# A convolution kernel: the second weight block's first sums moved ahead of the first unit's adds on GpSimd, and the first unit's silus moved back on ScalarE

## The chip, the cores and the metric

The kernel runs on one core of a Trainium2 chip. The core has TensorE (matmul; PE in the profile, its weight loads are PEld), VectorE (DVE), ScalarE (ACT), GpSimd (POOL) and SyncE (SP, which here issues nearly all DMAs). Each engine works through its own queue in order and waits on semaphores for the others. The metric is the device time of one execution in microseconds (us), as the median of several runs.

## What is computed

A one-dimensional convolution of width 3 over the sequence, a batch norm with given statistics, and a silu. B = 2 images, S = 2048 rows, C = 1024 channels in and out, bf16:

```
xp = jnp.pad(x, ((0, 0), (1, 1), (0, 0)))
y = sum(jnp.einsum('bsc,cd->bsd', xp[:, k:k + S, :], w[k]) for k in range(3))
y = (y - mean) * (g / jnp.sqrt(var + 1e-5)) + b
out = y * sigmoid(y)
```

## The kernel before, in words

The convolution is done by a fast algorithm of Winograd's kind. Six rows of the output (R = 6) come from eight products (NJ = 8), one for each of the points 0, 1, -1, 2, -2, 1/2, -1/2 and infinity, numbered 0 to 7 in this order. The image is transformed once by matmuls with a small constant matrix (`t_job`, L282 to L303; the results are cast from PSUM to SBUF by ScalarE or VectorE into `T_sb`). The weights are transformed block by block.

**Weights.** The 1024 output channels are 8 blocks `dc` of 128. For each block the three taps w0, w1, w2 lie in `raw[dc]`. `even_part` (L163) makes a sum e0 = w0 + w2, e1 = 4 w2 + w0 or e2 = 4 w0 + w2 in fp32. It does so on GpSimd in one `tensor_tensor` (L169) or on VectorE in one `scalar_tensor_tensor` with the factor 4 in it (L171). `transform_w` (L184, instruction at L190) makes on GpSimd the two signs of each pair: u0 = e0 +- w1, u1 = e1 +- 2 w1, u2 = e2 +- 2 w1. The doubled tap 2 w1 comes from `double_w` (L154), on ScalarE at L157, in a buffer named `w1x2`, of which there are two. Below, u1+ and u1- are the two signs of u1, and so on. u0 belongs to the points +-1, u1 to +-2 and u2 to +-1/2. Each sum and each sign is one instruction over 128 x 1024 elements.

`prepare_w(dc)` (L192) queues e0, u0+ and u0- at once, and leaves three jobs: the doubling for ScalarE (`act_work`), and e1 with u1, and e2 with u2 (`dve_work`), which `idle` takes off one by one at fixed places of later units. `prepare_first(0)` (L208) does the first block, all on GpSimd but the doubling.

**Units.** A unit is one block of output channels times one image; there are 16, in the order (block 0, image 0), (block 0, image 1), (block 1, image 0) and so on: unit 0, 1, 2, 3. Even units use PSUM banks 0 to 3, odd ones 4 to 7. Each of a unit's eight products is eight matmuls (one for each 128 input channels, L336), and is written here as (bank, number of the point), as in the call `self.product(q, j, ...)`; the bank is counted within the unit's four. A unit's order (`run`, L439) is (3,1), copy of bank 3; (0,3), copy of bank 0 times 4; (3,2), copy of bank 3; (0,4); (2,5), copy of bank 2; (2,6). The copies are ScalarE's (L347, L349). VectorE's combinations (`combine`, L354) turn the banks into the six output rows: t0, t1 and t2 from the low pair of banks, then four more behind (2,6). Two rows stand in banks 1 and 2, two in t1 (in SBUF), and two in banks 0 and 3, to which the products of point 0 and of infinity, (0,0) and (3,7), are added in the next unit. So, from unit 1 on, (3,7) of unit n runs between (2,5) and (2,6) of unit n + 1, and (0,0) behind (2,6). The silus (L359, ScalarE) read the banks and write `yT`; a DMA transpose (L524, SP) and stores follow.

**Places.** `run` calls `behind(n)` at numbered places: 1 behind the first copy, 4 behind (0,4), 5 behind the copy of bank 2 (the copy of point 5), 6 at the end. What is left of the unit before is given as a list of (place, function). As every engine's queue is in program order, this is a place in each engine's queue.

**Unit 0** (`run_first`, L384) is another: its (3,0) and (0,7) come first and are copied to `ends`, GpSimd adds these to t0 and t2 (L410, L411) once VectorE has made t0 and t2, and the image transforms of the second image run between its products. Right behind the two adds, `prepare_w(1)` (L412) puts e0, u0+ and u0- of block 1 into GpSimd's queue; at the unit's end `idle(act_work)` and `idle(dve_work)` (L421, L422) give ScalarE the doubling and VectorE e1. VectorE makes e2 in the middle of unit 1 (L469). Unit 0's silus are unit 1's affair (`rest_first`, L424): the two inner ones (t1 and banks 1 and 2) at place 4, the outer one (banks 0 and 3) at place 5. Unit 2 is the first to use block 1 and, after unit 0, the first to use banks 0 to 3 again.

Of the kernel before, what the change touches and what calls it, by code (L numbers as in the profile page):

```python
# [9 lines left out]
ALU = mybir.AluOpType  # L10
FP32 = mybir.dt.float32
BF16 = mybir.dt.bfloat16
# [3 lines left out]
P = 128  # L16
R = 6
# [9 lines left out]
def kernel(  # L27
# [10 lines left out]
    nc = tc.nc  # L38
    B, S, C = x.shape
    D = w.shape[2]  # L40
    CT, DC = C // P, D // P
# [9 lines left out]
    epool = ctx.enter_context(tc.tile_pool(name="epool", bufs=1))  # L51
    spool = ctx.enter_context(tc.tile_pool(name="spool", bufs=2))
# [12 lines left out]
    ps = pspool.tile([P, 8, 512], FP32, name="ps")  # L65
# [46 lines left out]
    def ends(e, size):  # L112
        return max(clock[e], clock["pe"] + 100.0) + cost[e][0] * size + cost[e][1]

    def busy(e, size):
        clock[e] = ends(e, size)
# [13 lines left out]
    raw, wts = {}, {}  # L130
# [3 lines left out]
    def load_w(pair, k, half=None):  # L134

        if (pair, "tile") not in raw:
            raw[pair, "tile"] = wpools[pair % 2].tile([P, 3, CT, 2, P], BF16, name=f"wch{pair % 2}")
        wch = raw[pair, "tile"]
        h0, h1 = (0, 2) if half is None else (half, half + 1)
        cols = slice((2 * pair + h0) * P, (2 * pair + h1) * P)  # L140
        nc.sync.dma_start(
            out=wch[:, k, :, h0:h1].rearrange("p c h d -> p c (h d)"), in_=w_all[:, k, :, cols]
        )
        clock["dma"] += 1400.0 * (h1 - h0)
        for h in range(2):
            raw[2 * pair + h] = wch[:, :, :, h]

    double, sums, act_work, dve_work = {}, {}, [], []

    def idle(work):  # L150
        if work:
            work.pop(0)()

    def double_w(dc, eng):  # L154
        t = spool.tile([P, CT, P], BF16, name="w1x2")
        if eng is nc.scalar:
            nc.scalar.mul(t, raw[dc][:, 1], 2.0)  # L157
            busy("act", CT * P)
        else:
            eng.tensor_scalar(t, raw[dc][:, 1], 2.0, 0.0, op0=ALU.mult, op1=ALU.add)  # L160
        double[dc] = t

    def even_part(dc, q, eng, by=None):  # L163

        w0, w2 = raw[dc][:, 0], raw[dc][:, 2]
        e = epool.tile([P, CT, P], FP32, name=f"e{q}")
        f, h = (w2, w0) if q == 1 else (w0, w2)
        if q == 0:
            eng.tensor_tensor(e, w0, w2, op=ALU.add)  # L169
        elif eng is nc.vector:  # L170
            eng.scalar_tensor_tensor(out=e, in0=f, scalar=4.0, in1=h, op0=ALU.mult, op1=ALU.add)  # L171
        else:
            t = spool.tile([P, CT, P], BF16, name="w1x2")
            if by is nc.scalar:
                by.mul(t, f, 4.0)
                busy("act", CT * P)
            else:
                by.tensor_scalar(t, f, 4.0, 0.0, op0=ALU.mult, op1=ALU.add)
            eng.tensor_tensor(e, t, h, op=ALU.add)
        if eng is nc.vector:  # L180
            busy("dve", CT * P)
        sums[dc, q] = e

    def transform_w(dc, q, signs=(0, 1)):  # L184

        o = double[dc] if q else raw[dc][:, 1]
        if (dc, q) not in wts:
            wts[dc, q] = upool.tile([P, 2, CT, P], BF16, name=f"u{q}")
        for i in signs:
            nc.gpsimd.tensor_tensor(wts[dc, q][:, i], sums[dc, q], o, op=(ALU.add, ALU.subtract)[i])  # L190

    def prepare_w(dc):  # L192

        even_part(dc, 0, nc.gpsimd)
        transform_w(dc, 0)

        def second():
            even_part(dc, 1, nc.vector)
            transform_w(dc, 1)

        def third():
            even_part(dc, 2, nc.vector)
            transform_w(dc, 2)

        act_work.append(lambda: double_w(dc, nc.scalar))
        dve_work.extend((second, third))

    def prepare_first(dc):  # L208
# [20 lines left out]

        return left  # L230

    prm = consts.tile([P, 4, DC], BF16, name="prm")
    scale = consts.tile([P, DC], FP32, name="scale")
    beta = consts.tile([P, DC], FP32, name="beta")
# [77 lines left out]
    class Unit:  # L312
# [54 lines left out]
        def first(self, between):  # L367

            self.product(0, 0, True, between)
            self.silu(0, self.bank[0])  # L370
# [10 lines left out]
            self.product(3, NJ - 1, True, between)  # L381
            self.silu(slice(0, R, R - 1), ps[:, self.b0:self.b0 + 4:3, self.lo:self.hi])

        def run_first(self, between, left, prepare):  # L384


            b0, b1, b2, b3 = self.bank
            sd = dpool.tile([P, 2, NB], FP32, name="sd")
            t0 = dpool.tile([P, 2, NB], FP32, name="t0")
            t2 = dpool.tile([P, 2, NB], FP32, name="t2")  # L390
            ends = dpool.tile([P, 2, NB], FP32, name="ends")
            self.y23 = t1 = ypool2.tile([P, 2, NB], FP32, name="t1")
            left()
            self.product(3, 0, False, between)
            self.copy(3, dst=ends[:, 0])
            self.product(0, NJ - 1, False, between)
            self.copy(0, dst=ends[:, 1])
            clock["pe"] = max(clock["pe"], T_FIRST)
            self.product(3, 1, False, between)
            pa = self.copy(3)  # L400
            self.product(0, 3, False, between)
            pb = self.copy(0, by=4.0)
            self.product(3, 2, True, between)
            self.copy(3, dst=sd[:, 0])
            self.combine(sd[:, 1], pa, 2.0, b3, ALU.subtract)
            self.product(0, 4, True, between)
            self.combine(b1, b0, -2.0, pb)
            for t, a in ((t0, -0.0125), (t2, -0.2), (t1, -0.05)):
                self.combine(t, self.low, a, sd)
            nc.gpsimd.tensor_tensor(t0[:, 0], t0[:, 0], ends[:, 0], op=ALU.add)  # L410
            nc.gpsimd.tensor_tensor(t2[:, 1], t2[:, 1], ends[:, 1], op=ALU.add)  # L411
            prepare_w(prepare)  # L412
            self.product(2, 5, False, between)
            pc = self.copy(2)
            between.rest()
            self.product(2, 6, True, between)
            self.combine(b3, b2, -0.5, pc)
            self.combine(self.low, self.high, -1.6, t0)
            self.combine(t1, self.high, -0.4, t1)
            self.combine(self.high, self.high, -0.1, t2)  # L420
            idle(act_work)  # L421
            idle(dve_work)  # L422

        def rest_first(self):  # L424

            return [
                (4, self.silu_inner),
                (5, lambda: self.silu(slice(0, R, R - 1), ps[:, self.b0:self.b0 + 4:3, self.lo:self.hi])),
            ]

        def rest(self, between, last=5, first=6):
# [118 lines left out]
    left = []  # L550
# [39 lines left out]
    between = Between()  # L590
# [3 lines left out]
    for i, (dc, bi) in enumerate(seq[:-1]):  # L594
        unit = Unit(dc, bi, i % 2 * 4)
        if i == 0:
            unit.run_first(between, left[0], 1)
        else:
            unit.run(
                between,  # L600
                prev.rest_first() if i == 1 else prev.rest(between, *((4, 5) if i >= len(seq) - 3 else (5, 6))),
                2 if i == 2 else dc + 2 if bi == 1 and 0 < dc < DC - 2 else None,
            )
        if i == 0:
            xwin_scope.close()
            olast = ctx.enter_context(tc.tile_pool(name="olast", bufs=3))
            wpools[1] = ctx.enter_context(tc.tile_pool(name="wpool1", bufs=1))
        if i in (0, 4, 8):
            for k in range(3):
                load_w(i // 4 + 1, k)  # L610
        if i == len(seq) - 2:
            prev.turn(olast, ((1, R), (0, 1)))
        elif prev:
            prev.turn()
        if before:
            before.store(late if i == len(seq) - 2 else ())
        before, prev = prev, unit
    before.store(late)
    dc, bi = seq[-1]
# [45 lines left out]
```

## Time and profile before

| | us |
|---|---|
| median of 3 runs | 192.54 |
| lowest, highest | 192.10, 192.76 |
| the profiled execution, its own time | 192.87 |
| its span, first to last instruction | 191.0 |
| TensorE busy | 178.2 (93%) |
| VectorE busy | 159.5 (84%) |
| GpSimd busy | 145.3 (76%) |
| ScalarE busy | 110.2 (58%) |

All durations come from the one profiled execution; 1.9 us of its time lie outside the span. Its mean granted TensorE clock is 0.999 of full speed. A row of a timeline shows start, length, engine, line, operation, tile written and tiles read, shape, and the count of instructions merged into it; brackets show the idle time ahead and what released the engine.

### The profile page before, as it was taken

What the parts mean: (1) busy time and instruction counts of PE and PEld (TensorE: products, weight loads), DVE (VectorE), ACT (ScalarE), POOL (GpSimd) and SP (SyncE); (2) the same over time, 40 slices, a digit from 0 to 9 for tenths busy, and PEclk for the clock granted to TensorE, in tenths of its full rate; (3) what the DMA queues carried; (4) which work ended last, traced back from release to release, by engine and by line L of the source; (5) the groups of instructions that cost most, each with busy time, mean ns of one, the idle gap of its engine ahead of it and who ended that gap; (6) DMA issues with size and microseconds to landing.
All of it is one profiled execution on the core that took longest, in us unless ns stands there. A gap on an engine that the chain in (4) does not pass through costs nothing.

```text
span 191.0 us, 3722 instructions
## 1 busy us (share of the span) xinstructions
PE 178.2 (93%) x1402; PEld 125.0 (65%) x1402; DVE 159.5 (84%) x214; ACT 110.2 (58%) x180; POOL 145.3 (76%) x86
## 2 busy tenths in 40 slices
PE   6969999998679999999999999999999999999991
PEld 2758688775336666666666666666666666669880
DVE  5548667899996999999998899889978897678781
ACT  3689698677118383638354745465455647363790
POOL 3377999179999779999999999999999973021122
PEclk9999999999999999999999999999999999999999
DMA  5999999056600939299597593994783958767935
GB/s 155 335 346 332 378 357 216 2 164 172 124 0 0 155 84 191 56 307 188 111 185 136 114 210 108 257 206 80 160 165 85 209 58 189 146 139 139 196 75 110
DMA packets 86958, 31.72 MB, mean 166 GB/s; under 512 B 73542, under 2 KB 82778, under 8 KB 86940
## 3 DMA queue, kind: packets, MB, share of 16 engines
q1 hardware_dynamic: 85820, 31.24, 71.3%
q10 hardware_dynamic: 864, 0.21, 0.5%
q8 instruction: 11, 0.18, 0.4%
q0 software_dynamic: 256, 0.03, 0.2%
q14 instruction: 7, 0.06, 0.1%
HBM read 14.82 MB, written 8.39 MB: 122 GB/s over the span
## 4 chain that ended last, share of the span: by engine, by line
PE 76%; POOL 6%; DMA 5%; DVE 5%; issue 3%; SPq 2%; ACT 1%; DVEq 0%; POOLq 0%
PE ps L336 71%; DMA xw<-in_x_dram 5%; PE ps L290 5%; POOL u L190 4%; DVE T_sb L303 4%; SPq L125 2%; POOL e L169 1%; ACT T_sb L301 1%; PE ps L495 1%; POOL t L411 0%; DVE t L354 0%; POOL t L410 0%; ACT yT L359 0%; DVEq L660 0%; DVE ps L354 0%
## 5 line engine op out<-in xcount | busy, mean ns | idle before, releaser
L336 PE MATMUL ps<-T_sb,u 128*128 128x342 bf16 (+2 forms) x816 | 120.7, 299 | 3.7 <-POOL u L190 2.5
L336 PEld LDWEIGHTS <-u 128*128 128x128 bf16 x816 | 76.4, 97 | 37.9 <-POOL u L190 4.2
L190 POOL TENSOR_TENSOR u<-e,w1x 128x1024 bf16<-128x1024 f32 x32 | 70.3, 2223 | 3.8 <-DVE e L171 2.5
L336 PE MATMUL ps<-T_sb,wch 128*128 128x342 bf16 (+2 forms) x272 | 43.0, 299 | 0.4 <-ACT T_sb L301 0.4
L190 POOL TENSOR_TENSOR u<-e,wch 128x1024 bf16<-128x1024 f32 x16 | 39.6, 2495 | 1.9 <-DMA wch<-in_w_dram 1.3
L359 ACT ACTIVATE yT<-ps,beta,scale 128x342 bf16<-128x342 f32 (+4 forms) x49 | 33.7, 719 | 11.0 <-PE ps L336 10.9
L354 DVE SCALAR_TENSOR_TENSOR t<-ps,sd 128x684 f32<-128x684 f32 (+2 forms) x51 | 39.1, 821 | 0.6
L347 ACT COPY pc<-ps 128x342 f32<-128x342 f32 (+2 forms) x34 | 14.5, 427 | 34.2 <-PE ps L336 33.5
L336 PEld LDWEIGHTS <-wch 128*128 128x128 bf16 x272 | 25.6, 97 | 11.8 <-issue 0.7
L171 DVE SCALAR_TENSOR_TENSOR e<-wch 128x1024 f32<-128x1024 bf16 x14 | 32.8, 2341 | 0.0
L303 DVE CAST T_sb<-ps 128x1008 bf16<-128x1008 f32 (+2 forms) x20 | 22.1, 1121 | 11.9 <-PE ps L290 11.8
L301 ACT CAST T_sb<-ps 128x1008 bf16<-128x1008 f32 (+2 forms) x30 | 24.9, 866 | 7.3 <-PE ps L290 7.1
L354 DVE SCALAR_TENSOR_TENSOR ps<-ps,t 128x684 f32<-128x684 f32 (+2 forms) x34 | 28.3, 832 | 0.7
L290 PE MATMUL ps<-rm,xw 128*128 128x168 bf16 (+2 forms) x272 | 25.3, 235 | 2.5 <-DMA xw<-in_x_dram 1.9
L290 PEld LDWEIGHTS <-xw 128*128 128x128 bf16 (+2 forms) x272 | 20.6, 99 | 8.6 <-DMA xw<-in_x_dram 3.3
L354 DVE SCALAR_TENSOR_TENSOR ps<-ps,pc 128x342 f32<-128x342 f32 (+2 forms) x34 | 16.8, 494 | 7.8 <-PE ps L336 6.7
L169 POOL TENSOR_TENSOR e<-wch 128x1024 f32<-128x1024 bf16 x7 | 16.9, 2412 | 0.0
L359 ACT ACTIVATE yT<-t,beta,scale 128x684 bf16<-128x684 f32 (+2 forms) x17 | 15.7, 925 | 0.0
L354 DVE SCALAR_TENSOR_TENSOR t<-ps,t 128x684 f32<-128x684 f32 (+2 forms) x17 | 13.9, 818 | 0.0
L349 ACT ACTIVATE pc<-ps 128x342 f32<-128x342 f32 (+2 forms) x17 | 7.5, 441 | 11.1 <-PE ps L336 8.3
L537 POOL DMA_DIRECT2D out_dram<-o x2 | 1.4, 712 | 15.7 <-DMA o<-yT 15.7
L347 ACT COPY sd<-ps 128x342 f32<-128x342 f32 (+2 forms) x17 | 7.3, 429 | 10.2 <-PE ps L336 10.2
(51 smaller groups left out, 55.9 us busy)
## 6 DMA issues: line engine op xcount, KB each, us to landing
xw<-in_x_dram SPq DMA_DIRECT2D x32, 256.0 KB
out_dram<-o SPq DMA_DIRECT2D x28, 192.0 KB
wch<-in_w_dram SPq DMA_DIRECT2D x9, 512.0 KB
out_dram<-o SPq DMA_DIRECT2D x14, 120.0 KB
wch<-in_w_dram SPq DMA_DIRECT2D x6, 256.0 KB
out_dram<-o SPq DMA_DIRECT2D x3, 128.0 KB
o<-yT SPq DMA_TRANSPOSE x15
out_dram<-o SPq DMA_DIRECT2D x12, 7.5 KB
```

The source lines that it names most:

```text
L125: nc.sync.dma_start(out=xw[0:hi - lo, :], in_=x[bi, lo:hi, :])
L169: eng.tensor_tensor(e, w0, w2, op=ALU.add)
L171: eng.scalar_tensor_tensor(out=e, in0=f, scalar=4.0, in1=h, op0=ALU.mult, op1=ALU.add)
L190: nc.gpsimd.tensor_tensor(wts[dc, q][:, i], sums[dc, q], o, op=(ALU.add, ALU.subtract)[i])
L290: nc.tensor.matmul(v[:, q, c], lhsT=xw[0:rows, (c0 + c) * P:(c0 + c + 1) * P], rhs=mat[0:rows, :, 0:n], start=True, stop=True,)
L301: nc.scalar.copy(dst, src)
L303: nc.vector.tensor_copy(dst, src)
L336: nc.tensor.matmul(self.bank[q], lhsT=lhsT, rhs=T_sb[self.bi][:, ct, j, nsl], start=not add and ct == 0, stop=ct == CT - 1, skip_group_che ...
L347: nc.scalar.copy(dst, self.bank[q])
L349: nc.scalar.mul(dst, self.bank[q], by)
L354: nc.vector.scalar_tensor_tensor(out=out, in0=in0, scalar=scalar, in1=in1, op0=ALU.mult, op1=op1)
L359: nc.scalar.activation(self.yT[:, rows, self.lo:self.hi], src, ACT.Silu, bias=beta[:, dc:dc + 1], scale=scale[:, dc:dc + 1])
```

## The change

Three things move, all for block 1, whose weights unit 2 uses first. A new function `prepare_second(1)` takes the place of `prepare_w(1)` and returns four jobs.

- GpSimd: e0 and u0+ stand in front of the two adds of L410 and L411, and u0- behind them.
- e1 is made on GpSimd, as one `tensor_tensor` of w0 and a buffer `g` = 4 w2; ScalarE makes `g` at the end of unit 0, where it made the doubled tap. The buffer is of the name `w1x2`, as the doubled tap's is. VectorE makes e2 at the end of unit 0, where it made e1, and nothing for block 1 in unit 1.
- At place 1 of unit 1 (behind its first copy) come the doubling on ScalarE, then e1, u1 and u2 on GpSimd.
- Unit 0's silus in unit 1: the inner two from place 4 to place 5, the outer one from place 5 to place 6.

```
+    def prepare_second(dc):
+        w0, w2 = raw[dc][:, 0], raw[dc][:, 2]
+        g = spool.tile([P, CT, P], BF16, name="w1x2")
+
+        def first():
+            even_part(dc, 0, nc.gpsimd)
+            transform_w(dc, 0, (0,))
+
+        def times4():
+            nc.scalar.mul(g, w2, 4.0)
+            busy("act", CT * P)
+
+        def second():
+            double_w(dc, nc.scalar)
+            sums[dc, 1] = epool.tile([P, CT, P], FP32, name="e1")
+            nc.gpsimd.tensor_tensor(sums[dc, 1], g, w0, op=ALU.add)
+            transform_w(dc, 1)
+            transform_w(dc, 2)
+
+        return first, times4, lambda: even_part(dc, 2, nc.vector), second
...
+            dc, (first, times4, third, second) = following
+            first()
             nc.gpsimd.tensor_tensor(t0[:, 0], t0[:, 0], ends[:, 0], op=ALU.add)
             nc.gpsimd.tensor_tensor(t2[:, 1], t2[:, 1], ends[:, 1], op=ALU.add)
-            prepare_w(prepare)
+            transform_w(dc, 0, (1,))
...
-            idle(act_work)
-            idle(dve_work)
+            times4()
+            third()
+            self.second = second
...
-                (4, self.silu_inner),
-                (5, lambda: self.silu(slice(0, R, R - 1), ps[:, self.b0:self.b0 + 4:3, self.lo:self.hi])),
+                (1, self.second), (5, self.silu_inner),
+                (6, lambda: self.silu(slice(0, R, R - 1), ps[:, self.b0:self.b0 + 4:3, self.lo:self.hi])),
...
-            unit.run_first(between, left[0], 1)
+            unit.run_first(between, left[0], (1, prepare_second(1)))
```

More of the change, by code (lines that the diff above doesn't have):

```diff
@@ L382, in both, with run_first @@
             self.silu(slice(0, R, R - 1), ps[:, self.b0:self.b0 + 4:3, self.lo:self.hi])
-        def run_first(self, between, left, prepare):
+        def run_first(self, between, left, following):
             b0, b1, b2, b3 = self.bank
```

## The prediction

> **What bounds the kernel now.** I read the page's shares first, then the chain of waits in order of time, then the timeline of one engine after the other around the place where the chain leaves TensorE.
>
> ```profile
> PE 178.2 (93%) x1402; PEld 125.0 (65%) x1402; DVE 159.5 (84%) x214; ACT 110.2 (58%) x180; POOL 145.3 (76%) x86
> ...
> PE 76%; POOL 6%; DMA 5%; DVE 5%; issue 3%; SPq 2%; ACT 1%; DVEq 0%; POOLq 0%
> ```
>
> TensorE is busy for 93% of the span and carries 76% of the chain that ended last. GpSimd's 6% is the largest share of another engine. The chain in order of time ends its GpSimd part like this (start, length, what):
>
> ```profile
> 53.80 2.13 POOL u L190
> 55.94 0.05 issue
> 55.98 122.33 PE ps L336 x856
> ```
>
> From 55.98 us on TensorE runs 122.33 us without a break in the chain. Whatever time is won or lost ahead of 55.98 should therefore move the end by the same amount, and nothing behind it looks late today. TensorE's own timeline there (start, length, count; in brackets the idle time before it and its releaser):
>
> ```profile
> 38.82 7.13 PE L336 MATMUL ps<-T_sb,u 128*128 128x342 bf16 x48
> 46.54 2.48 PE L336 MATMUL ps<-T_sb,u 128*128 128x342 bf16 x16 [0.59 <-ACT pc L347]
> 50.83 2.49 PE L336 MATMUL ps<-T_sb,u 128*128 128x342 bf16 x16 [1.80 <-POOL u L190]
> 53.90 1.33 PE L336 MATMUL ps<-T_sb,u 128*128 128x342 bf16 x8 [0.58 <-ACT sd L347]
> 55.98 1.34 PE L336 MATMUL ps<-T_sb,u 128*128 128x342 bf16 x8 [0.75 <-POOL u L190]
> 57.16 1.32 PE L336 MATMUL ps<-T_sb,wch 128*128 128x342 bf16 x8
> ...
> 60.64 5.98 PE L336 MATMUL ps<-T_sb,u 128*128 128x342 bf16 x40
> ```
>
> A product is 8 matmuls. Three products lie between 57.16 and 60.64, so one takes 1.16 us from start to start; the printed lengths are longer because the ends of pipelined matmuls are modelled. The 48 matmuls from 38.82 are unit 0's last product and unit 1's first five. At 46.54 come unit 1's (2,6) and, at 46.54 + 1.16 = 47.70, unit 2's (3,1), the first product with the second block's weights. Then (0,3) could start at 48.86 and starts at 50.83: 1.97 lost. (0,4) could start at 50.83 + 2.32 = 53.15 and starts at 53.90: 0.75 lost. (2,5) could start at 55.06 and starts at 55.98: 0.92 lost. Together **3.64 us**. GpSimd explains all three:
>
> ```profile
> 30.08 4.22 POOL L190 TENSOR_TENSOR u<-e,w1x 128x1024 bf16<-128x1024 f32 x2
> 39.53 0.92 POOL L410 TENSOR_TENSOR t<-t,ends 128x342 f32<-128x342 f32 x1 [5.23 <-DVE t L354]
> 40.40 0.92 POOL L411 TENSOR_TENSOR t<-t,ends 128x342 f32<-128x342 f32 x1
> 41.27 2.13 POOL L169 TENSOR_TENSOR e<-wch 128x1024 f32<-128x1024 bf16 x1
> 43.48 5.20 POOL L190 TENSOR_TENSOR u<-e,wch 128x1024 bf16<-128x1024 f32 x2
> 48.65 9.38 POOL L190 TENSOR_TENSOR u<-e,w1x 128x1024 bf16<-128x1024 f32 x4
> 57.98 2.12 POOL L169 TENSOR_TENSOR e<-wch 128x1024 f32<-128x1024 bf16 x1
> ```
>
> The first block is finished at 34.30. GpSimd then stands still for 5.23 us until VectorE's t0, adds the ends, and only at 41.27 begins the second block: e0, u0+, u0- (up to 48.65), then u1+, u1-, u2+, u2-. u1+ ends at about 50.8 and (0,3) starts at 50.83. The chain shows u2+ beginning at 53.80, so u1- ended there, and (0,4) starts at 53.90; ACT is named in that row, but its sd copy is of another bank. u2+ ends at 55.93 and (2,5) starts at 55.98.
>
> **The change, part by part.** (a) e0 and u0+ go into the 5.23 us hole: 2 x 2.13 from 34.30 ends at 38.6, 0.9 before t0 is there. Their input must have landed; in the table by stretches (the last two columns are DMA share and GB/s):
>
> ```profile
> 33.00:34.00 1.00, 1.00 (x14) 0.86 (x12) 0.60 (x1) 1.00 (x3) 1.00 (x1) 1.00 0.13 22
> 34.00:35.00 1.00, 1.00 (x14) 0.89 (x13) 1.00 (x3) 0.70 (x1) 0.30 (x1) 1.00 0.01 3
> ```
>
> The queue runs dry in these two stretches, and the taps 0 and 2, which e0 reads, were issued ahead of tap 1, which only u0+ reads. So e0 can start at 34.3. If both ran at 3.1 us, the longer kind of the pair at 43.48 (5.20 - 2.13), they would end at 40.5, one us into the adds; L410 would end at 41.4 and L411 at 42.3. VectorE reads the two sums here:
>
> ```profile
> 41.46 0.88 DVE L354 SCALAR_TENSOR_TENSOR ps<-ps,t 128x684 f32<-128x684 f32 x1
> ...
> 43.03 0.87 DVE L354 SCALAR_TENSOR_TENSOR ps<-ps,t 128x684 f32<-128x684 f32 x1
> ```
>
> t0 is needed at 41.46 and t2 at 43.03, so the cost is nothing either way; later still, each us would be a us for VectorE, which has no gap there.
>
> (b) Behind the adds GpSimd has u0- (41.27 to 43.4), then e1, which it now makes itself from ACT's 4 x w2, then u1+, u1-, u2+, u2-. That is one instruction more on GpSimd, +2.13, against 4.26 moved forward. The VectorE work around it:
>
> ```profile
> 43.80 2.89 DVE L171 SCALAR_TENSOR_TENSOR e<-wch 128x1024 f32<-128x1024 bf16 x1
> ...
> 49.92 1.93 DVE L171 SCALAR_TENSOR_TENSOR e<-wch 128x1024 f32<-128x1024 bf16 x1
> ```
>
> At 43.80 VectorE now makes e2 in place of e1, at the same price; the one at 49.92 goes, and unit 1's last combines come 1.93 earlier, which only loosens what unit 2 waits for. A VectorE sum next to a GpSimd sum lengthens both:
>
> ```profile
> L171 DVE SCALAR_TENSOR_TENSOR e<-wch x14: 1216/2338/3046, 43.8 to 152.0; 128x1024 f32<-128x1024 bf16 x14
> ```
>
> These sums take 1.22 us at the shortest and 2.89 here (minimum, median, maximum in ns), and GpSimd's second sign took 3.1. So I charge GpSimd one such collision, 1.0: e1 to 45.6, u1+ to 48.7, u1- to 50.8, u2+ to 52.9, u2- to 55.0. The Trainium skill says why, in "SBUF — State Buffer", section "Who interferes with whom": VectorE with two SBUF inputs and a reading GpSimd hold a shared port exclusively for a whole instruction. The trace agrees: the 2.89 is the rest of GpSimd's running sign plus some 1.2. By a plain sharing of bandwidth both would merely be stretched, and the u times would be up to 1.0 earlier; that changes only the margins of rival B.
>
> (c) ACT. Its timeline:
>
> ```profile
> 40.24 1.07 ACT L157 ACTIVATE w1x<-wch 128x1024 bf16<-128x1024 bf16 x1
> 41.72 0.45 ACT L347 COPY pc<-ps 128x342 f32<-128x342 f32 x1 [0.41 <-PE ps L336]
> 42.51 0.46 ACT L349 ACTIVATE pc<-ps 128x342 f32<-128x342 f32 x1 [0.34 <-PE ps L336]
> 43.71 0.45 ACT L347 COPY sd<-ps 128x342 f32<-128x342 f32 x1 [0.75 <-PE ps L336]
> 44.05 0.96 ACT L359 ACTIVATE yT<-t,beta,scale 128x684 bf16<-128x684 f32 x1
> 44.91 0.91 ACT L359 ACTIVATE yT<-ps,beta,scale 128x684 bf16<-128x684 f32 x1
> 46.05 0.45 ACT L347 COPY pc<-ps 128x342 f32<-128x342 f32 x1 [0.22 <-PE ps L336]
> 46.39 0.93 ACT L359 ACTIVATE yT<-ps,beta,scale 128x684 bf16<-128x684 f32 x1
> 49.06 0.45 ACT L347 COPY pc<-ps 128x342 f32<-128x342 f32 x1 [1.75 <-PE ps L336]
> ```
>
> The multiplication by 4 takes the place of the doubling at 40.24, at 1.07. The doubling moves behind the copy of 41.72: it starts at 42.06 (0.34 behind, as 46.39 stands to 46.05) and ends near 43.1, so the 4x copy runs from 43.0 to 43.5 instead of from 42.51. Queued behind the doubling are that copy and then all of unit 1. Unit 1's (0,4) overwrites what the 4x copy reads and starts at 38.82 + 4 x 1.16 = 43.46: a stall of 0 to 0.15, I take 0.05. Its input buffers are free since 34.30.
>
> (d) **The silus are the price.** Unit 2 uses unit 0's banks, and its (3,1) writes bank 3, which unit 0's outer silu reads. Today that silu runs 46.39 to 47.32, just ahead of 47.70. After the change the two inner silus stand behind the copy of 46.05 and the outer one behind them: 46.39, 47.25 and 48.11 at the spacing of 44.05 and 44.91, ending at 48.11 + 0.93 = 49.04. TensorE restarts 0.04 after an ACT end (46.50 to 46.54), so (3,1) starts at 49.08 instead of 47.70: a **new wait of 1.38** in front of unit 2. Queued behind it is the whole of TensorE. Unit 2's first copy on ACT follows (3,1), so it is not held.
>
> The store of unit 0 is released by the same silu, so SP's transpose is issued some 1.7 later; the next thing in SP's queue needs unit 1's silus, a whole unit later, so nobody waits for that.
>
> **Sum**, starts of unit 2: (3,1) 49.08, (0,3) 50.24, (3,2) 51.40, (0,4) 52.56, (2,5) 53.72, the next unit-1 product 54.88, (2,6) 56.04. The signs they need are ready at 48.7, 43.4, 50.8, 52.9 and 55.0 for (0,3), (3,2), (0,4), (2,5) and (2,6): margins of 0.8 us or more. So (2,5) starts at 53.72 instead of 55.98: 3.64 - 1.38 = **2.26 won**, less 0.05: 2.2. Behind it GpSimd takes up the third block at 55.0 instead of 57.98, and VectorE's sums for it hang on the combines, which move with TensorE; I see nothing late next. The profiled execution would go from 192.87 (span 191.0) to 190.7; it lies 0.33 above the median of 192.54, so for the median **190.3**.
>
> **The rivals.** *A, the silus do not hold TensorE* (they run faster one behind another, or unit 2 gets in front). Then unit 2 starts at 47.70 and GpSimd's u2+ at 52.9 lets (2,5) go at 52.95 instead of 52.34: 55.98 - 52.95 = 3.0 won, 189.5. For it: only 1.38 us have to vanish. Against: three silus of 0.86 spacing in one queue, and a bank that is read.
>
> *B, GpSimd decides again*: slow e0 and u0+ (1.0 late) and a second collision (1.0) put u2+ at 54.9 instead of 52.9. (2,5) then waits 1.2, and 1.0 is won: 191.5. For it: the margin is 0.8. Against: a VectorE sum that collided has gone, and the casts between 34 and 39 ran beside GpSimd sums of 2.1 before.
>
> *C, slower*: the doubling waits. Its buffer is one of two of the name that 4 x w2 also takes. If it got the buffer of 4 x w2, ACT would stand in front of the 4x copy until e1 is done at 45.6; the copy would end at 47.0, and unit 1's (0,4) would start at 47.05 instead of 43.46. The silus follow 3.6 later, and unit 2's (2,5) stands at 53.72 + 3.6 = 57.3, 1.3 behind today: 193.9. It decides from 2.3 us of delay. Against: the first block's doubled tap was last read at 34.30, so a buffer should be free.
>
> **How the numbers follow.** Forecast 0.66, A 0.12, B 0.13 (0.05 of it within 0.3%), C 0.09. About 0.3%, 0.6 us, is what a measurement of this kernel can tell from no change. Faster is 0.66 + 0.12 + 0.08 = 0.86, the same 0.05, slower 0.09. The range takes in A and B with 0.2 of scatter below A: 189.3 to 191.5.
>
> **What would show it.** In the changed profile: e0 and one u sign at 34.3 to 38.6 on GpSimd; the L410 wait down to about 1 us; three silus in a row on ACT from 46.4; a TensorE wait of about 1.4 for ACT's yT at L359 ahead of unit 2; no wait for GpSimd's u behind it; the unbroken stretch from about 49.1. A wait for u in unit 2 means B, a start at 47.7 means A, an idle ACT in front of L157 means C. A wait behind 58.4, where unit 3 now starts, would mean that I missed what is late next.

## The result, and the profile after

The changed kernel takes 190.49 us (median of 6 runs, 190.22 to 191.14) against 192.58 us (6 runs) before: a ratio of **0.9898, 95% interval 0.9878 to 0.9918**, or 2.0 us less (1.6 to 2.3). The prediction was 190.3, with 189.3 to 191.5.

TensorE's timeline of the changed kernel, at the place that bounded the kernel before (line 336 of before is line 359 here, and the silus' line 359 is 382):

```profile
38.64 7.17 PE L359 MATMUL ps<-T_sb,u 128*128 128x342 bf16 x48
46.35 1.32 PE L359 MATMUL ps<-T_sb,u 128*128 128x342 bf16 x8 [0.53 <-ACT pc L370]
48.83 5.97 PE L359 MATMUL ps<-T_sb,u 128*128 128x342 bf16 x40 [1.16 <-ACT yT L382]
54.63 1.32 PE L359 MATMUL ps<-T_sb,wch 128*128 128x342 bf16 x8
```

The three waits for GpSimd's u are gone. In their place stands one wait, of 1.16 us, for a silu's yT, ahead of unit 2's first product at 48.83. Behind it five products run without a gap. The chain in order of time has no GpSimd left:

```profile
46.30 0.55 ACT yT L382
46.85 0.20 issue
47.05 1.73 ACT yT L382 x2
48.78 0.04 issue
48.83 126.89 PE ps L359 x888
```

GpSimd's timeline shows the new order. e0 and u0+ fill the hole that was 5.23 us, and 0.96 of it is left:

```profile
34.05 2.12 POOL L169 TENSOR_TENSOR e<-wch 128x1024 f32<-128x1024 bf16 x1
36.25 2.12 POOL L190 TENSOR_TENSOR u<-e,wch 128x1024 bf16<-128x1024 f32 x1
39.34 0.92 POOL L435 TENSOR_TENSOR t<-t,ends 128x342 f32<-128x342 f32 x1 [0.96 <-DVE t L377]
40.21 0.92 POOL L436 TENSOR_TENSOR t<-t,ends 128x342 f32<-128x342 f32 x1
41.08 2.13 POOL L190 TENSOR_TENSOR u<-e,wch 128x1024 bf16<-128x1024 f32 x1
43.17 2.13 POOL L249 TENSOR_TENSOR e<-w1x,wch 128x1024 f32<-128x1024 bf16 x1
45.38 9.26 POOL L190 TENSOR_TENSOR u<-e,w1x 128x1024 bf16<-128x1024 f32 x4
```

And ScalarE's row shows the doubling (L157) behind unit 1's first copy, and three silus behind the copy of bank 2, the last of which ends at 48.77:

```profile
41.53 0.45 ACT L370 COPY pc<-ps 128x342 f32<-128x342 f32 x1 [0.41 <-PE ps L359]
41.87 1.06 ACT L157 ACTIVATE w1x<-wch 128x1024 bf16<-128x1024 bf16 x1
42.83 0.45 ACT L372 ACTIVATE pc<-ps 128x342 f32<-128x342 f32 x1
43.53 0.45 ACT L370 COPY sd<-ps 128x342 f32<-128x342 f32 x1 [0.25 <-ACT pc L372]
45.85 0.45 ACT L370 COPY pc<-ps 128x342 f32<-128x342 f32 x1 [1.88 <-PE ps L359]
46.19 0.96 ACT L382 ACTIVATE yT<-t,beta,scale 128x684 bf16<-128x684 f32 x1
47.05 1.72 ACT L382 ACTIVATE yT<-ps,beta,scale 128x684 bf16<-128x684 f32 x2
```

**A measure for the experiments.** How early unit 1's (2,6) starts differs by some tenths of a us from one profile to the next (46.54 before, 46.35 here), and in one of them by more than 1 us. So I also compare the *stretch* from the start of unit 1's (2,6) to the start of (3,7) in unit 2. It holds six products, 6 x 1.16 = 6.96 us with no wait at all. Before it was 57.16 - 46.54 = 10.62; now it is 54.63 - 46.35 = 8.28.

### The profile page after: what moved, and what is told of

Same layout as the page of the kernel before. It is cut to its first block, busy times and chain, and to the rows that moved or that the text cites. A ratio compares the mean times of both kernels' runs of the same rounds, so it can differ in the third digit from the quotient of the medians.

```text
span 188.5 us, 3723 instructions
## 1 busy us (share of the span) xinstructions
PE 177.0 (94%) x1402; PEld 124.9 (66%) x1402; DVE 154.2 (82%) x213; ACT 111.0 (59%) x181; POOL 146.4 (78%) x87
## 4 chain that ended last, share of the span: by engine, by line
PE 83%; DMA 5%; DVE 4%; ACT 3%; SPq 2%; issue 1%; DVEq 0%
PE ps L359 77%; PE ps L313 5%; DMA xw<-in_x_dram 5%; DVE T_sb L326 4%; SPq L125 2%; ACT yT L382 2%; ACT T_sb L324 1%; PE ps L521 1%; SPq L141 0%; DVEq L686 0%; ACT pc L370 0%; DVE sd L377 0%; DVE o L522 0%; DVEq L326 0%
## 5 line engine op out<-in xcount | busy, mean ns | idle before, releaser
L190 POOL TENSOR_TENSOR u<-e,wch 128x1024 bf16<-128x1024 f32 x16 | 38.7, 2435 | 1.8 <-DMA wch<-in_w_dram 1.2
L313 PE MATMUL ps<-rm,xw 128*128 128x168 bf16 (+2 forms) x272 | 24.8, 233 | 3.1 <-DMA xw<-in_x_dram 2.6
L171 DVE SCALAR_TENSOR_TENSOR e<-wch 128x1024 f32<-128x1024 bf16 x13 | 26.7, 2051 | 0.0
L313 PEld LDWEIGHTS <-xw 128*128 128x128 bf16 (+2 forms) x272 | 20.1, 97 | 8.9 <-DMA xw<-in_x_dram 3.9
L377 DVE SCALAR_TENSOR_TENSOR sd<-pc,ps 128x342 f32<-128x342 f32 (+2 forms) x17 | 8.3, 486 | 6.8 <-ACT sd L370 6.7
```

The source lines that it names most:

```text
L313: nc.tensor.matmul(v[:, q, c], lhsT=xw[0:rows, (c0 + c) * P:(c0 + c + 1) * P], rhs=mat[0:rows, :, 0:n], start=True, stop=True,)
L377: nc.vector.scalar_tensor_tensor(out=out, in0=in0, scalar=scalar, in1=in1, op0=ALU.mult, op1=op1)
```

## The experiments

The theory: GpSimd's late start on block 1 cost TensorE 3.64 us; the early start removes that, and the late outer silu, which reads a bank that unit 2 overwrites, gives 1.2 to 1.4 us back. The rivals are these: the win has to do with VectorE's missing sum or with e1 on GpSimd; the silus' new place is free, or costs because ScalarE is loaded, not because of the bank; the costs of the parts simply add up. Differences are the ratio, less 1, times the median of before on the same chip.

| run | ratio to before, 95% interval | us against before | stretch, us |
|---|---|---|---|
| the changed kernel | 0.9898 (0.9878 to 0.9918) | -2.0 | 8.28 |
| e1_silus_early | 0.9835 (0.9814 to 0.9856) | -3.2 | 7.60 |
| e6_outer_first | 0.9846 (0.9823 to 0.9868) | -3.0 | 8.09 |
| e2_silus_only | 1.0005 (0.9991 to 1.0019) | +0.1 | 10.67 |
| e3_e0_ahead_only | 0.9838 (0.9817 to 0.9860) | -3.1 | 7.36 |
| e4_e1_on_gpsimd_only | 1.0132 (1.0102 to 1.0162) | +2.5 | 12.75 |
| e5_e0_ahead_silus_late | 0.9866 (0.9849 to 0.9883) | -2.6 | 8.28 |
| e7_changed_plus_one_sign | 0.9939 (0.9917 to 0.9961) | -1.2 | 8.76 |
| e8_silus_early_plus_one_sign | 0.9910 (0.9895 to 0.9925) | -1.7 | 8.76 |
| e9_e4_with_fillers | 1.0065 (1.0051 to 1.0079) | +1.3 | 11.78 |
| changed_again | 0.9888 (0.9868 to 0.9909) | -2.2 | 8.29 |
| e3_again | 0.9849 (0.9822 to 0.9875) | -2.9 | 7.36 |

**Silus back at their old places**

```
-                (1, self.second), (5, self.silu_inner),
-                (6, lambda: self.silu(slice(0, R, R - 1), ...)),
+                (1, self.second), (4, self.silu_inner),
+                (5, lambda: self.silu(slice(0, R, R - 1), ...)),
```

> The changed kernel with unit 0's silus back at their old places (inner at 4, outer at 5); all else as changed. Theory (the GpSimd order wins 3.64 us and the late outer silu gives 1.2 to 1.4 of it back): the outer silu ends ahead of unit 2's first product again, the wait of 1.16 us for yT goes, and GpSimd's u2+, which ended near 52.45 in the changed profile, lets (2,5) start about 0.9 us earlier than now: 189.6 us. Rival (the gain comes with VectorE's missing sum and the silus' place costs nothing, or early silus hold up ScalarE's copies behind the moved doubling): 190.5 or slower.

Measured: 3.2 us faster than before, 1.2 more than the change wins. TensorE's timeline of this run:

```profile
45.90 5.97 PE L359 MATMUL ps<-T_sb,u 128*128 128x342 bf16 x40 [0.59 <-ACT pc L370]
52.32 1.34 PE L359 MATMUL ps<-T_sb,u 128*128 128x342 bf16 x8 [0.46 <-POOL u L190]
53.50 1.32 PE L359 MATMUL ps<-T_sb,wch 128*128 128x342 bf16 x8
```

The wait for yT is gone: five products run from 45.90, and only (2,5) waits 0.46 us for u2+. The part of the change that moves the silus is a loss.

**The outer silu first**

```
-                (1, self.second), (5, self.silu_inner),
-                (6, lambda: self.silu(slice(0, R, R - 1), ...)),
+                (1, self.second), (5, lambda: self.silu(slice(0, R, R - 1), ...)),
+                (5, self.silu_inner),
```

> The changed kernel with the outer silu ahead of the two inner ones, all three at place 5. ScalarE has the same work behind the same copy, in another order. Theory (it is the bank that the outer silu reads, not ScalarE's load): the outer silu ends near 47.1, unit 2's first product starts without a wait, (2,5) then waits for u2+ as in the run with early silus: 189.6 us. Rival (ScalarE's three silus in a row hold up the next copies and products whatever their order): 190.5 us.

Measured: 3.0 us faster than before, 1.0 more than the change wins. ScalarE still has its three silus in a row, and unit 2's first product no longer waits. The first fence is of ScalarE, the second of TensorE, the third of GpSimd in this run:

```profile
46.00 0.93 ACT L382 ACTIVATE yT<-ps,beta,scale 128x684 bf16<-128x684 f32 x1
46.82 0.95 ACT L382 ACTIVATE yT<-t,beta,scale 128x684 bf16<-128x684 f32 x1
```

```profile
46.16 2.48 PE L359 MATMUL ps<-T_sb,u 128*128 128x342 bf16 x16 [0.53 <-ACT pc L370]
48.90 3.65 PE L359 MATMUL ps<-T_sb,u 128*128 128x342 bf16 x24 [0.26 <-POOL u L190]
53.07 1.34 PE L359 MATMUL ps<-T_sb,u 128*128 128x342 bf16 x8 [0.52 <-POOL u L190]
```

```profile
35.35 2.12 POOL L169 TENSOR_TENSOR e<-wch 128x1024 f32<-128x1024 bf16 x1
```

The 16 matmuls from 46.16 are unit 1's (2,6) and unit 2's (3,1) back to back. So it is the outer silu's bank that holds TensorE, not ScalarE's load. The waits for u that are left come from GpSimd, which in this profile reached e0 at 35.35 instead of 34.05; the profiled run is the slowest of this kernel's five (189.84, median 189.34).

**The silus' move alone**, on the kernel before:

```
-                (4, self.silu_inner),
-                (5, lambda: self.silu(slice(0, R, R - 1), ...)),
+                (5, self.silu_inner),
+                (6, lambda: self.silu(slice(0, R, R - 1), ...)),
```

> The kernel before, with only unit 0's silus moved back (inner to 5, outer to 6). Theory: unit 2's first product is held 1.4 us by the outer silu, but its second waits for GpSimd's u1+ until 50.8 anyway, so the wait only changes its name: 192.5 us, no change. Rival (the costs add up part by part): 1.4 us slower, 193.9 us.

Measured: 1.0005 of before, no change. TensorE's timeline shows why:

```profile
46.50 1.32 PE L336 MATMUL ps<-T_sb,u 128*128 128x342 bf16 x8 [0.53 <-ACT pc L347]
48.98 1.32 PE L336 MATMUL ps<-T_sb,u 128*128 128x342 bf16 x8 [1.16 <-ACT yT L359]
50.83 2.50 PE L336 MATMUL ps<-T_sb,u 128*128 128x342 bf16 x16 [0.53 <-POOL u L190]
```

The wait for yT is there, 1.16 us as in the changed kernel, but (0,3) starts at 50.83 as before: the wait for u1+ shrank from 1.80 to 0.53 and ended at the same instant. The same edit costs nothing here and about a microsecond in the changed kernel. Costs did not add up; the later of the two releasers decides.

**Only e0 and u0+ ahead of the adds**; everything else as before:

```
+            even_part(prepare, 0, nc.gpsimd)
+            transform_w(prepare, 0, (0,))
             nc.gpsimd.tensor_tensor(t0[:, 0], t0[:, 0], ends[:, 0], op=ALU.add)
             nc.gpsimd.tensor_tensor(t2[:, 1], t2[:, 1], ends[:, 1], op=ALU.add)
             prepare_w(prepare)
```

For block 1, `prepare_w` then queues only u0- at once.

> The kernel before, with only e0 and u0+ of block 1 moved ahead of GpSimd's two adds; e1 stays on VectorE, the doubling and the silus stay where they were. Theory (what counts is that GpSimd's row of sums starts in its idle 5.2 us): GpSimd is then free at 43.4, VectorE's e1 no longer collides and ends near 45.0, u1+ at 47, u1- at 49, e2 by 50.3, u2+ at 52.4, u2- at 54.5; unit 2 waits at most some tenths: about 3.3 us faster than before, 189.2 us. Rival (e1 on GpSimd is what the gain needs, since VectorE's e1 and e2 come too late): at most half of the gain, 191.3 us or slower.

Measured: 3.1 us faster than before, and 2.9 in the second pair of runs. This one move of two GpSimd instructions wins more than the whole change. TensorE runs unit 1's (2,6) and four products of unit 2 without a break, and only (2,5) waits, 0.22 us for u2+:

```profile
46.10 5.96 PE L339 MATMUL ps<-T_sb,u 128*128 128x342 bf16 x40 [0.59 <-ACT pc L350]
52.29 1.34 PE L339 MATMUL ps<-T_sb,u 128*128 128x342 bf16 x8 [0.22 <-POOL u L190]
```

VectorE's e1 in this run, and then GpSimd from u0- on:

```profile
43.36 1.22 DVE L171 SCALAR_TENSOR_TENSOR e<-wch 128x1024 f32<-128x1024 bf16 x1
```

```profile
40.81 2.13 POOL L190 TENSOR_TENSOR u<-e,wch 128x1024 bf16<-128x1024 f32 x1
44.72 4.22 POOL L190 TENSOR_TENSOR u<-e,w1x 128x1024 bf16<-128x1024 f32 x2 [1.78 <-DVE e L171]
50.10 4.22 POOL L190 TENSOR_TENSOR u<-e,w1x 128x1024 bf16<-128x1024 f32 x2 [1.16 <-DVE e L171]
```

GpSimd stands idle when VectorE makes e1, so that takes 1.22 us in place of 2.89. GpSimd now waits 1.78 and 1.16 for VectorE's sums, 2.94 together, against the 2.13 plus a collision of 1.0 that e1 costs it in the changed kernel. It comes out even: from the start of u0- to the end of the four signs GpSimd takes about 13.5 us in both (40.81 to 54.32 here, 41.08 to 54.64 in the changed kernel). E1 on GpSimd isn't needed.

**Only e1 on GpSimd**: `first()` behind the two adds, silus at their old places, the rest as changed.

> The kernel before with only e1 moved to GpSimd (4 x w2 and the doubling on ScalarE and e2 on VectorE as in the change), while e0 and u0+ stay behind the two adds and the silus at their old places. Theory (only the start in GpSimd's idle 5.2 us wins; e1 on GpSimd costs its 2.1 us): GpSimd's row is u1+ to about 52.9, u1- to 55.0, u2+ to 57.1, u2- to 59.2, so (2,5) starts near 57.15 instead of 55.98: 1.2 us slower than before. Rival (relief of VectorE is part of the gain): not slower than before.

Measured: 2.5 us slower (2.0 to 3.1), where 1.2 was expected. The direction is the theory's; the size is twice it. TensorE's timeline and then the table by stretches (columns: stretch, its length, busy us and number of instructions of PE, PEld, DVE, ACT and POOL, granted clock, DMA share, GB/s):

```profile
45.75 2.49 PE L359 MATMUL ps<-T_sb,u 128*128 128x342 bf16 x16 [0.59 <-ACT pc L370]
52.16 6.50 PE L359 MATMUL ps<-T_sb,u 128*128 128x342 bf16 x32 [3.92 <-POOL u L190]
58.50 1.32 PE L359 MATMUL ps<-T_sb,wch 128*128 128x342 bf16 x8
```

```profile
50.00:52.00 2.00, 0.00 (x0) 0.00 (x0) 2.00 (x3) 0.00 (x0) 2.00 (x1) 1.00 0.39 72
52.00:53.00 1.00, 0.84 (x5) 0.57 (x6) 0.04 (x1) 0.00 (x0) 1.00 (x2) 0.80 0.00 0
53.00:54.00 1.00, 1.00 (x5) 0.49 (x4) 0.00 (x0) 0.00 (x0) 1.00 (x1) 0.50 0.00 0
54.00:55.00 1.00, 1.00 (x5) 0.57 (x4) 0.00 (x0) 0.46 (x1) 1.00 (x2) 0.50 0.00 0
55.00:56.00 1.00, 1.00 (x5) 0.48 (x4) 0.00 (x0) 0.00 (x0) 1.00 (x1) 0.50 0.00 0
56.00:57.00 1.00, 1.00 (x8) 0.69 (x7) 0.11 (x1) 0.44 (x1) 1.00 (x2) 0.99 0.00 0
```

TensorE waits 3.92 us for u1+. Soon after it starts again its granted clock falls to 0.50 and stays there until 56; the table has five matmuls in each us there and eight in the one behind it, at 0.99. The profile shows no wait inside the 32 matmuls, yet from start to start they take 6.34 us, where four products take 4.64. The 1.70 us more are what 3.4 us at half the clock come to. The Trainium skill has this in "TensorE: Matmul & The Clock Gate", section "Part 1": an idle window of about 3.4 us halves TensorE's clock until it has been busy for about as long. This trace agrees: 3.92 us idle, then some 3.4 us at 0.50, while the waits of up to 1.80 us in the kernel before left the clock at 1.00. The six runs of this kernel point the same way: the three longest (195.13 to 196.15) have a mean granted clock of 0.975 or 0.976, the three shortest (194.05 to 194.46) 0.984 to 0.991. The profiled run is the shortest.

To see whether the clock is the missing part, the next run fills the idle time of e4 with two products whose result is not used:

```
             behind(1)
+            if (self.dc, self.bi) == (1, 0):
+                for n in range(2 * CT):
+                    nc.tensor.matmul(
+                        b1, lhsT=wts[1, 0][:, 0, n % CT], rhs=T_sb[0][:, n % CT, 1, sl],
+                        start=n % CT == 0, stop=n % CT == CT - 1,
+                    )
             self.product(0, 3, False, between)
```

> The run with only e1 moved to GpSimd, plus 16 matmuls more on TensorE (two products of u0+ into bank 1, which unit 2 overwrites later; their result is not used), in the place where TensorE stood idle for 3.92 us and after which its granted clock read 0.50 for 3.4 us. They end ahead of the u1+ that TensorE waits for. Theory (1.2 us of that run's loss are GpSimd's row, the rest is the halved clock that follows the long idle time): the clock stays at 1.00 and the run is about 1.2 us slower than before in place of 2.5. Rival (all of the loss is GpSimd's row): unchanged at 2.5 us slower, or more.

Measured: 1.3 us slower than before (1.0 to 1.5), half of the loss. TensorE's timeline and two stretches of this run:

```profile
48.27 2.49 PE L485 MATMUL ps<-T_sb,u 128*128 128x342 bf16 x16
52.38 3.65 PE L359 MATMUL ps<-T_sb,u 128*128 128x342 bf16 x24 [1.62 <-POOL u L190]
56.55 1.34 PE L359 MATMUL ps<-T_sb,u 128*128 128x342 bf16 x8 [0.51 <-POOL u L190]
```

```profile
52.00:54.00 2.00, 1.61 (x12) 1.09 (x13) 0.25 (x1) 0.20 (x1) 2.00 (x2) 1.00 0.00 0
54.00:56.00 2.00, 2.00 (x15) 1.16 (x12) 0.51 (x1) 0.70 (x2) 2.00 (x2) 1.00 0.00 0
```

Sixteen matmuls whose result nobody reads made the kernel 1.3 us faster than without them; the clock stays at 1.00 in these stretches, and the mean of each of the five runs is 0.993 or more. What is left, 1.3 us (1.16 by the stretch), is GpSimd's row, as worked out for the run without them (1.2). By the stretches of the two profiled runs the halved clock cost 0.97 (12.75 against 11.78), less than its 1.70, since at full clock (2,5) waits 0.51 for u2+ instead.

**e0 and u0+ ahead, and the silus late** (the two edits of e3 and e2 together):

> The run with only e0 and u0+ ahead of the adds, and unit 0's silus moved back as in the change. Theory: the outer silu holds unit 2's first product for 1.2 us again; GpSimd's waits behind it vanish, so this is about 1.1 us slower than the run without the silus' move and equal to the changed kernel: 2.0 us faster than before. Rival (the late silus are free as they were on the kernel before): 3.0 us faster than before.

Measured: 2.6 us faster than before (2.3 to 2.9), between the two expectations. Its profile is clear where the time is not:

```profile
45.44 1.32 PE L339 MATMUL ps<-T_sb,u 128*128 128x342 bf16 x8 [0.53 <-ACT pc L350]
47.92 5.96 PE L339 MATMUL ps<-T_sb,u 128*128 128x342 bf16 x40 [1.16 <-ACT yT L362]
53.72 1.32 PE L339 MATMUL ps<-T_sb,wch 128*128 128x342 bf16 x8
```

The same wait of 1.16 for yT, no wait for u, and a stretch of 8.28 as in the changed kernel, 0.92 more than in e3. The medians of these two runs differ by 0.5, and the intervals of their ratios overlap.

**One GpSimd instruction more ahead of the adds**: `transform_w(dc, 0, (0,))` twice in `first()`, on the changed kernel and on the one with early silus.

> The changed kernel with one GpSimd instruction more, u0+ written twice ahead of the two adds: 2.1 us more work on GpSimd, of which 0.96 fits into the idle time that is left there, so its row ends 1.2 later. Theory (the silu holds TensorE and GpSimd has about 1 us to spare behind it): at most 0.3 us slower than the changed kernel, 1.7 to 2.0 us faster than before. Rival (GpSimd's row sets the end as before): 1.2 us slower than the changed kernel, 0.8 us faster than before.

> The same u0+ written twice ahead of the adds, in the version with the silus at their old places. Theory (there GpSimd's u2+ is what TensorE waits for): the whole 1.2 us or, where GpSimd's 0.96 of idle time was gone already, up to 2.1 us comes through: 1.0 to 1.9 us faster than before instead of 3.1. Rival (GpSimd no longer matters once its row starts early): 3 us faster than before, as without it.

Measured: with early silus 1.7 us faster than before instead of 3.2, so 1.5 of the 2.1 us come through, inside what the theory gave. On the changed kernel the same instruction costs 0.8 us (1.2 faster than before instead of 2.0), more than the theory's 0.3 and less than the rival's 1.2. The interval, 0.7 to 1.6 faster than before, takes in the rival's 0.8 and not the theory's 1.7 to 2.0, so by the times alone the theory missed. TensorE in the changed kernel with the extra sign:

```profile
48.67 4.80 PE L360 MATMUL ps<-T_sb,u 128*128 128x342 bf16 x32 [1.16 <-ACT yT L383]
53.78 1.34 PE L360 MATMUL ps<-T_sb,u 128*128 128x342 bf16 x8 [0.31 <-POOL u L190]
```

The silu still comes first and u2+ then adds 0.31; the stretch grows by 0.48. That profile is of the fastest of six runs (190.58, median 191.31); what the slower ones spend more isn't settled. In the profile the size of the miss can be followed: in the changed kernel u2+ ended at 52.56 and (2,5) could start at 53.47, so GpSimd had 0.9 to spare where I had put about 1, and here u2+ ends 1.16 later while TensorE runs 0.16 earlier. That leaves some 0.4, near the 0.48.

**The changed kernel and e3 on one chip**

> The changed kernel unaltered, to stand beside the next one on one chip: 2.0 us faster than before.

> The run with only e0 and u0+ ahead of the adds, unaltered. Theory (the silus' move and e1 on GpSimd are not needed): 3.0 us faster than before and 1.0 us faster than the changed kernel beside it. Rival (the difference between the two was that of two chips): the same as the changed kernel.

Measured: 2.2 and 2.9 us faster than before. Over both pairs of runs the changed kernel stands at 0.9898 and 0.9888, e3 at 0.9838 and 0.9849. In the second pair alone the two intervals overlap a little (0.9868 and 0.9875); the profiles agree to 0.01 with the first ones (8.28 and 8.29; 7.36 and 7.36). The versions that beat both kernels are e3, e1 and e6, which can't be told from one another by their intervals.

## Why the prediction was right

- *What bounds the kernel*: right. The 3.64 us of lost starts were GpSimd's: starting its row earlier left no wait for u in the changed kernel, 0.22 us in e3, 0.46 in e1 and 0.78 in e6, and the time won before 55.98 went through to the end.
- *(a) e0 and u0+ in the hole, at no cost*: right, 34.05 to 38.37 against 34.3 to 38.6 predicted; the wait at the adds went to 0.96 (about 1 was said). E3 shows that this step is the whole win.
- *(b) e1 on GpSimd, one collision*: right in the times: the four signs end at 54.6 (55.0 predicted), 9.26 us for four, one of them longer. What I did not ask is whether this part is needed. It isn't (e3), and by itself it costs about 1.2 us of GpSimd's row and another 1.3 through the clock (e4, e9).
- *(c) the doubling on ScalarE, 0.05*: right in size, though it did not reach the end. The 4x copy follows at 42.83 and the 48 matmuls take 7.17 instead of 7.13. From their start to (2,6) it is 7.77 in e1 against 7.72 before, but 7.71 in the changed kernel: the silus' move takes about as much off in the same place (7.66 in e2), which the prediction did not count. Rival C, ScalarE stuck at the doubling, didn't come: L157 starts 0.34 behind the copy.
- *(d) the silus*: right as a mechanism (e1, e6, e2) and in size: unit 2 was to start at 49.08, which is 48.90 by the changed profile's clock, 0.18 earlier at the 48 matmuls. It started at 48.83, which is 1.32 behind the 47.51 at which it could have started (1.38 predicted). The price in the whole kernel is 1.2 between the changed kernel and e1, and 1.0 against e6; on top of e3 it is 0.5 by the times and 0.92 by the stretch.
- *Rival A* priced what the kernel would do without the silus' wait: 3.0 us won, with (2,5) waiting for u2+. E1 is that case: 3.2 won, and (2,5) waits 0.46.
- *Rival B*, GpSimd deciding again from 2 us of lateness, did not come. E7 shows it begin at 1.2 us, where the prediction had a margin of 0.8.
- *The sum*: 2.2 predicted, 2.0 measured (1.6 to 2.3), 2.34 in the profiled stretch. The profiled run, 190.22, is the fastest of the six. Why the median is some tenths above it I did not settle; GpSimd's start, which moved by 1.3 us between two profiles, is a candidate, argued only.

## What to carry to other kernels

When an engine that starves TensorE has an idle hole ahead of its late work, move work into the hole first and measure that alone; here moving two instructions gave 3 us, and the other two parts of the change gave nothing or took about 1 us. Before moving a reader of a PSUM bank back in its queue, ask which product overwrites the bank next: the same move was free while another wait ended later, and cost 0.5 to 1.2 us once that wait was gone. Read lost time from start to start, not from the printed idle times: the three waits were printed with 3.13 us in all and had cost 3.64.

## What was not expected of the hardware

A wait of 3.92 us on TensorE cost 1.3 us more than itself (0.97 by the stretch of the profiled runs), because the granted clock was 0.50 for some 3.4 us after it; sixteen useless matmuls in the gap, which cut the wait to 1.62, took that loss away. VectorE's sum took 1.22 us with GpSimd idle and 2.89 beside it, so an engine's idle time can shorten another engine's instruction. Which of the two pays depended here on which began first: in the changed kernel GpSimd's e1 began at 43.17 and took 2.13, and VectorE's sum from 43.62 took 2.76; in e6 VectorE's sum began at 43.43 and took 1.21, and GpSimd's e1 from 43.48 took 3.15.
